# Fifteen computed softmax features per head in place of sixteen, in a linear-attention kernel

## The chip, the cores and the metric

The kernel runs on one core of one Trainium2 chip. TensorE (PE) does matrix products, VectorE (DVE), ScalarE (ACT) and GpSimd (POOL) work on rows of data, SyncE (SP) issues DMAs, and each engine takes its instructions in the order in which they were written for it. The metric is device time in microseconds.

## The reference

One sequence of 2048 rows of width 512 passes through two layers, each a linear attention and a gated MLP, with layer norms and residuals. What matters here is the feature map of the attention: 32 heads of 16 dimensions, and per head a softmax over 16 features of `q @ w_phi` and one over the negated values.

```python
pq = jnp.einsum("bhsd,hdf->bhsf", q, w_phi)
pk = jnp.einsum("bhsd,hdf->bhsf", k, w_phi)
phi_q = jnp.concatenate([_softmax(pq, axis=-1), _softmax(-pq, axis=-1)], axis=-1)
phi_k = jnp.concatenate([_softmax(pk, axis=-1), _softmax(-pk, axis=-1)], axis=-1)
kv = jnp.einsum("bhsf,bhsd->bhfd", phi_k, v)
z  = jnp.einsum("bhsf->bhf", phi_k)
num = jnp.einsum("bhqf,bhfd->bhqd", phi_q, kv)
den = jnp.einsum("bhqf,bhf->bhq", phi_q, z)[..., None] + 1e-6
o = num / den
```

Both layers use the same weights. The MLP is `(relu(x @ W_gate) * (x @ W_up)) @ W_down` with a width of 1376.

## The kernel before

The 2048 rows are 16 tiles of 128. Activations in bf16, weights and all intermediate tiles stay in SBUF. `w_phi` is folded into the key and query weights at the start (`fold`): `Wk2` and `Wq2` are the products of the projection and of a block-diagonal `Wblk`, so that one product per tile gives the logits of all 32 heads, 512 columns. A softmax does not change when a constant is subtracted from its logits, and `centre` subtracts the mean of `w_phi` over the features ahead of the fold.

**A key tile** (`Keys.begin`, `finish`, `scale`): four matmuls of 512 columns into a PSUM bank (line 571; the first tile of the first layer goes by another way, lines 562 and 567), two exponentials on ScalarE, of the logits and of their negatives, into a buffer `ek` (574), four matmuls for the values (577), one VectorE sum over groups of 16 into `sk` (582), logarithm and exponential of minus the logarithm on ScalarE as a reciprocal (591, 594), a scaling of the features in place by it, on POOL or VectorE (534), and eight matmuls `kvz` that add to the state, with features as weights and values as moving data (606).

**A query tile** (`query`): four matmuls of 512 columns (633), two exponentials (636), a sum into `sq` (639), logarithm and exponential (644, 646) of the positive half's sums only, the ratio of the negative sum to the positive one (650), on POOL or VectorE, a scaling of the positive half by it (654), on POOL or VectorE, and a transposing DMA on SP's queue into `fq`. The common factor of both halves cancels in num / den. `attend` then multiplies `fq` with the masked state `R` (670), divides (677 to 684), transposes, projects (693) and adds the residual (697). `mlp` follows (matmuls at 746, 770 and 810).

The order of the work isn't computed when the program is built: `ORDER` lists all steps in the order in which they are issued, `PLACE` says for each step that could run on two engines which it takes, `IDLE` puts in filler matmuls, and `SLOTS` gives the buffer of each tile that a step takes from a pool. `arrange` only replays them. There are 21 `ek` buffers for keys and queries alike, six PSUM banks `b`. The costs that stand beside each step aren't used when the lists are replayed. A step that overwrites a buffer waits for its last reader.

The program's parts follow each other loosely: constants and fold to some 10 us, keys and queries of the first layer to some 57 us, then attention and MLP of the first layer in blocks of tiles, with the second layer's keys and queries threaded in between to some 240 us, and the second layer's MLP to the end.

Of the kernel before, what the change touches and what calls it, by code (L numbers as in the profile page):

```python
# [8 lines left out]
P = 128  # L9
D = 512  # L10
# [13 lines left out]
GE = HG * (DH + 1)  # L24
EPS = 1e-5
# [117 lines left out]
class K:  # L143
# [24 lines left out]
)  # L168
IDLE = (
# [107 lines left out]
def kernel(  # L277
# [26 lines left out]
    Wk2, Wq2 = new("Wk2", [NB, D]), new("Wq2", [NB, D])  # L304
# [20 lines left out]
    p_ek = p_eq = pool("ek", 21, [NG, 2, GQ])  # L325
# [71 lines left out]
    c_id = op("POOL", (900, 900), 0, lambda: make_identity(nc, ident[:]), name="ident")  # L397
    c_eps = op("DVE", DVE0, 0, lambda: nc.vector.memset(eps[:], EPS), name="eps")
# [11 lines left out]
    def centre():  # L410
        nc.vector.tensor_reduce(out=cmean[:], in_=wf[:], axis=AX.X, op=Alu.add)
        nc.vector.scalar_tensor_tensor(out=wf[:], in0=cmean[:].unsqueeze(2).to_broadcast([P, NB, DH]),
                                       scalar=-1.0 / DH, in1=wf[:], op0=Alu.mult, op1=Alu.add)

    def blocks(e):
        e.tensor_tensor(
            out=Wblk[:].rearrange("p b (j f) -> p b j f", f=DH),
            in0=wf[:].unsqueeze(2).to_broadcast([P, NB, HB, DH]),
            in1=Mf[:].unsqueeze(1).unsqueeze(3).to_broadcast([P, NB, HB, DH]), op=Alu.mult)

    c_cen = op("DVE", (400, 500), 20, centre, [l_wf], name="wcen", port=True)
    c_blk = op("DVE", (640, 740), 20, lambda: blocks(nc.vector), [c_m, c_cen], name="Wblk", port=True,
               alt=("POOL", (1016, 1058), lambda: blocks(nc.gpsimd), 3))
    c_mg = op("DVE", DVE0, 15000, lambda: nc.vector.tensor_tensor(
        out=Mg[:], in0=Mf[:, 0:HG], in1=Mf[:, HG:HB], op=Alu.add), [c_m], name="Mg")
# [20 lines left out]
    def fold(w, dst, loaded, due, step, engs, by_dma=False):  # L446
# [17 lines left out]
        for m in range(NB):  # L464
            ps = Buf(p_b)
            f = op("PE", mm(4, 128), due + step + m, lambda m=m, ps=ps: [nc.tensor.matmul(
                ps.t[:, b * P:(b + 1) * P],
                lhsT=wT.t[:, m, b * P:(b + 1) * P] if by_dma else wT.t[:, b, m * P:(m + 1) * P], rhs=Wblk[:, b, :],
                start=True, stop=True) for b in range(NB)], [turned[m], c_blk], [ps], [wT], name="fold")
            done.append(evac(engs[m % 2], due + step + m, lambda m=m: dst[:, m, :], lambda ps=ps: ps.t[:], [f], (),  # L470
                             [ps], "W2"))
# [58 lines left out]
    def halves(name, ek, out, scale, engs, due, after, takes, uses):  # L530
        parts = []

        def phi(e, lo, n):
            e.tensor_tensor(  # L534
                out=out().rearrange("p g s (h f) -> p (g s h) f", f=DH)[:, lo:lo + n],
                in0=ek.t[:].rearrange("p g s (h f) -> p (g s h) f", f=DH)[:, lo:lo + n],
                in1=scale(lo, n).unsqueeze(2).to_broadcast([P, n, DH]), op=Alu.mult)
        for k, e in enumerate(engs):
            ways = {"DVE": ("DVE", dve(512), lambda k=k: phi(nc.vector, k * H, H), 1),
                    "POOL": ("POOL", (1016, 1058), lambda k=k: phi(nc.gpsimd, k * H, H), 3)}  # L540
            _, cost, f, _ = ways[e]
            parts.append(op(e, cost, due, f, after, [] if k else takes, uses + (takes if k else []), name=name,
                            port=ways[e][3], alt=ways["POOL" if e == "DVE" else "DVE"]))
        return parts

    class Keys:
# [9 lines left out]
        def begin(self, sk, row, t, due, due_v, due_z, xT, phi_eng, v_eng="ACT"):  # L556
# [3 lines left out]
            if self.l == 0 and t < PLAIN:  # L560
                kT, tp = Buf(p_gu), Buf(p_b)
                k = op("PE", (960, 1130, 16), due, lambda: [nc.tensor.matmul(
                    tp.t[:, e * P:(e + 1) * P], lhsT=wk[:, b, e * P:(e + 1) * P], rhs=xnTA[c][:, i, b, :],
                    start=(b == 0), stop=(b == NB - 1)) for e in range(NB) for b in range(NB)],
                    [xT] + l_wk, [tp], name="KT")
                k = evac("DVE", due, lambda: kT.t[:, 0, :], lambda: tp.t[:], [k], [kT], [tp], "kT")
                k = op("PE", mm(4, 128), due, lambda: [nc.tensor.matmul(
                    kp.t[:, b * P:(b + 1) * P], lhsT=kT.t[:, 0, b * P:(b + 1) * P], rhs=Wblk[:, b, :],
                    start=True, stop=True) for b in range(NB)], [k, c_blk], [kp], [kT], name="K")
            else:  # L570
                k = op("PE", mm(4, 512), due, lambda: [nc.tensor.matmul(  # L571
                    kp.t[:], lhsT=xnTA[c][:, i, b, :], rhs=Wk2[:, b, :], start=(b == 0), stop=(b == NB - 1))
                    for b in range(NB)], [xT] + k_fold, [kp], name="K")
            e = [op("ACT", act(512), due, lambda s=s: nc.scalar.activation(  # L574
                out=ek.t[:, :, s, :], in_=kp.t[:].rearrange("p (g e) -> p g e", e=GQ), func=AF.Exp, scale=1.0 - 2.0 * s), [k], [ek] if s == 0 else [],
# [7 lines left out]
                out=sk.t[:, row, :], in_=ek.t[:].rearrange("p g s (h f) -> p (g s h) f", f=DH), axis=AX.X, op=Alu.add),  # L583
# [5 lines left out]
        def finish(self, begun):  # L589
            n, sk, due = len(begun), begun[0][2], begun[-1][5]  # L590
            a = op("ACT", RLN[n - 1], due, lambda: nc.scalar.activation(
                out=sk.t[:, 0:n, :], in_=sk.t[:, 0:n, :], func=AF.Ln, scale=1.0), [b[0] for b in begun], (), [sk],
                name="lnk")
            a = op("ACT", REXP[n - 1], due, lambda: nc.scalar.activation(  # L594
                out=sk.t[:, 0:n, :], in_=sk.t[:, 0:n, :], func=AF.Exp, scale=-1.0), [a], (), [sk], name="rk")
            for row, b in enumerate(begun):
                self.scale(a, row, *b[1:])

        def scale(self, a, row, v, sk, ek, vx, due, due_z, phi_eng):
            a = halves("phi", ek, lambda: ek.t[:], lambda lo, n: sk.t[:, row, lo:lo + n], PHI[phi_eng], due, [a], [],  # L600
                       [ek, sk])

            def kvz():
                for g in range(NG):
                    b = g % NB
                    nc.tensor.matmul(self.bufs.t[:, g, 0:GV],  # L606
                                     lhsT=ek.t[:, g, :, :].rearrange("p s e -> p (s e)"), rhs=vx.t[:, g, 0:GV],
# [22 lines left out]
    def query(l, t, due, xT, behind, key):  # L630
        c, i = t // C, t % C
        qp, ek, sq, fq = Buf(p_a), Buf(p_eq), Buf(p_sq), Buf(p_fq)
        q = op("PE", mm(4, 512), due, lambda: [nc.tensor.matmul(  # L633
            qp.t[:], lhsT=xnTA[c][:, i, b, :], rhs=Wq2[:, b, :], start=(b == 0), stop=(b == NB - 1))
            for b in range(NB)], [xT] + q_fold, [qp, ek], name="Q", follow=key)
        e = [op("ACT", act(512), due, lambda s=s: nc.scalar.activation(  # L636
            out=ek.t[:, :, s, :], in_=qp.t[:].rearrange("p (g e) -> p g e", e=GQ), func=AF.Exp, scale=1.0 - 2.0 * s),
            [q], (), [qp, ek], name="Eq") for s in range(2)]
        a = op("DVE", SUM16, due, lambda: nc.vector.tensor_reduce(  # L639
            out=sq.t[:], in_=ek.t[:].rearrange("p g s (h f) -> p (g s h) f", f=DH), axis=AX.X, op=Alu.add),  # L640
# [4 lines left out]
            out=pos(), in_=pos(), func=AF.Ln, scale=1.0), [a], (), [sq], name="lnq")  # L645
# [3 lines left out]
        def ratio(e):  # L649
            e.tensor_tensor(out=pos(), in0=pos(), in1=neg(), op=Alu.mult)  # L650

        def scale(e):
            v = ek.t[:, :, 0, :].rearrange("p g (h f) -> p g h f", f=DH)
            e.tensor_tensor(out=v, in0=v, in1=pos().unsqueeze(3).to_broadcast([P, NG, HG, DH]), op=Alu.mult)  # L654
        a = op("POOL", (212, 253), due, lambda: ratio(nc.gpsimd), [a], [], [ek, sq], name="rat", port=3,
               alt=("DVE", DVE0, lambda: ratio(nc.vector), 1))
        a = op("POOL", (1016, 1058), due, lambda: scale(nc.gpsimd), [a], [], [ek, sq], name="phq", port=3,
               alt=("DVE", dve(512), lambda: scale(nc.vector), 1))
        a = op("SP", XWIDE, due, lambda: nc.sync.dma_start_transpose(
            out=fq.t[:], in_=ek.t[:].rearrange("p g s e -> p (g s e)")), [a], [fq], [ek], name="fq", move=1450)  # L660
# [268 lines left out]
```

## Time and profile before

| what | value |
|---|---|
| median of three timed runs | 374.3 us (373.25 to 374.6) |
| span of the profiled execution, first to last instruction | 371.3 us |
| median less that span (starting and ending work around it) | 3.0 us |
| granted TensorE clock | 1.000 |
| TensorE busy | 363.7 us |
| VectorE busy | 273.1 us |
| ScalarE busy | 201.8 us |
| POOL busy | 97.6 us |
| key matmuls, line 571 | 120 records, 30.6 us |
| query matmuls, line 633 | 122 records, 31.5 us |
| exponentials, lines 574 and 636 | 64 of 642 ns, 64 of 637 ns (mean) |
| logarithms, lines 591 and 644 | 32 of 319 ns, 32 of 252 ns (mean) |

The profiled execution has no total of its own beside its span, so the 3.0 us are the difference to the median of the timed runs. Busy is the time in which at least one instruction of an engine is under way. Instructions of one engine overlap, so that a mean duration can include waiting for the one ahead, and is longer than the time for which the engine is held. Some matmul records are missing from the trace: 124 key matmuls and 128 query matmuls of 512 columns were issued.

In the rows of the profile, `L571` is line 571 of the kernel before, `b<-Wk,xnTA` says that a tile of pool `b` is written from `Wk` and `xnTA`, `x120` is a count, and an arrow at the end names what ended the idle time ahead of an instruction.

### The profile page before, as it was taken

To read this page: it belongs to the slowest core of one execution; us is meant where nothing else is said; L and a number is where in the kernel's file an instruction comes from. 1 tells how busy PE (TensorE), PEld (TensorE's weight loads), DVE (VectorE), ACT (ScalarE), POOL (GpSimd) and SP (SyncE) were. 2 spreads that over 40 slices of the span, in tenths; PEclk is the share of its full clock that TensorE was granted. 3 is DMA by queue.
4 is the path that set the end of the run, shared out by engine and by line. 5 is a ranking of instruction groups with operands and counts; after the bars stand their busy time and mean duration, and the time that the engine had idled before them with its cause. 6 is when DMAs were issued, how large, how long until landed. Compare 5 with 4: busy or idle time off the path is not lost.

```text
span 371.3 us, 7447 instructions
## 1 busy us (share of the span) xinstructions
PE 363.7 (98%) x2799; PEld 217.4 (59%) x2845; DVE 273.1 (74%) x578; ACT 201.8 (54%) x549; POOL 97.6 (26%) x123
## 2 busy tenths in 40 slices
PE   8999999999999999999999999999999999999996
PEld 5454557776455454545566655687755454457484
DVE  6999999988798966849969489799976373233253
ACT  5999999661644750586274455874434226403130
POOL 4599974610030116005212174141000000000000
PEclk9999999999999999999999999999999999999999
DMA  8998676686653501203411210488851102010213
GB/s 247 185 236 154 230 129 128 128 158 116 92 99 58 99 15 31 40 18 64 87 31 34 57 28 3 58 131 125 142 104 45 28 0 44 0 45 0 79 52 98
DMA packets 93925, 31.73 MB, mean 85 GB/s; under 512 B 85345, under 2 KB 92865, under 8 KB 93889
## 3 DMA queue, kind: packets, MB, share of 16 engines
q1 hardware_dynamic: 93088, 30.98, 41.4%
q8 instruction: 22, 0.36, 0.4%
q10 hardware_dynamic: 800, 0.28, 0.3%
q14 instruction: 15, 0.11, 0.1%
HBM read 8.44 MB, written 2.10 MB: 28 GB/s over the span
## 4 chain that ended last, share of the span: by engine, by line
PE 85%; ACT 9%; DVE 2%; issue 1%; DMA 1%; POOL 0%; SPq 0%; DVEq 0%; ACTq 0%
PE b L770 38%; PE b L810 20%; PE b L693 7%; PE b L571 5%; PE b L577 5%; PE b L633 4%; ACT ek L574 3%; PE b L746 3%; PE q L670 2%; ACT ek L636 2%; PE q L606 1%; DMA X<-in_A_x_dram 1%; DVE ek L534 1%; PE b L485 1%; ACT vext L438 1%
## 5 line engine op out<-in xcount | busy, mean ns | idle before, releaser
L770 PE MATMUL b<-xnTB,wgu 128*128 128x128 bf16 (+2 forms) x1200 | 152.5, 279 | 0.1
L770 PEld LDWEIGHTS <-wgu 128*128 128x128 bf16 x1200 | 97.4, 98 | 47.2 <-issue 0.3
L774 ACT ACTIVATE gu<-b 128x512 bf16<-128x512 f32 (+1 forms) x83 | 47.7, 582 | 90.7 <-PE b L770 85.4
L810 PE MATMUL b<-wd,hT 128*128 128x512 bf16 (+3 forms) x342 | 83.5, 372 | 1.2
L534 POOL TENSOR_TENSOR ek<-ek,sk 128x512 bf16<-128x512 bf16 x48 | 52.1, 1109 | 74.1 <-ACT sk L594 69.4
L810 PEld LDWEIGHTS <-hT 128*128 128x128 bf16 (+1 forms) x363 | 34.2, 98 | 34.0 <-DVE hT L787 0.3
L787 DVE TENSOR_TENSOR hT<-gu,b 128x512 bf16<-128x512 bf16 (+1 forms) x44 | 28.6, 658 | 30.0 <-ACT gu L774 13.6
L574 ACT ACTIVATE ek<-b 128x512 bf16<-128x512 f32 x64 | 38.5, 642 | 9.1 <-PE b L571 8.9
L636 ACT ACTIVATE ek<-b 128x512 bf16<-128x512 f32 x64 | 37.5, 637 | 7.8 <-PE b L633 7.8
L639 DVE TENSOR_REDUCE sq<-ek 128x64 f32<-128x1024 bf16 x32 | 38.5, 1211 | 4.1 <-ACT ek L636 4.1
L582 DVE TENSOR_REDUCE sk<-ek 128x64 f32<-128x1024 bf16 x32 | 38.2, 1206 | 2.9 <-ACT ek L574 2.7
L654 POOL TENSOR_TENSOR ek<-ek,sq 128x512 bf16<-128x512 bf16 x26 | 27.8, 1077 | 43.8 <-DVE sq L650 33.1
L778 DVE TENSOR_TENSOR hT<-gu 128x512 bf16<-128x512 bf16 (+1 forms) x39 | 16.9, 435 | 22.5 <-ACT gu L789 22.5
L817 DVE SCALAR_TENSOR_TENSOR X<-b,rsB,X 128x512 bf16<-128x512 f32 (+2 forms) x33 | 23.7, 730 | 12.4 <-PE b L810 12.2
L693 PE MATMUL b<-wo,oT 128*128 128x512 bf16 x118 | 31.2, 379 | 1.1 <-ACT oT L438 0.4
L633 PE MATMUL b<-Wq,xnTA 128*128 128x512 bf16 x122 | 31.5, 379 | 0.4
L577 PE MATMUL b<-wv,xnTA 128*128 128x512 bf16 x123 | 31.1, 379 | 0.3
L571 PE MATMUL b<-Wk,xnTA 128*128 128x512 bf16 x120 | 30.6, 379 | 0.1
L697 DVE SCALAR_TENSOR_TENSOR X<-b,X 128x512 bf16<-128x512 f32 x32 | 21.8, 686 | 6.2 <-PE b L693 5.9
L789 ACT CAST gu<-b 128x512 bf16<-128x512 f32 (+1 forms) x39 | 21.9, 573 | 6.8 <-PE b L770 6.6
L684 DVE TENSOR_TENSOR o<-q,rd 128x512 bf16<-128x512 f32 x32 | 22.0, 687 | 1.3 <-ACT rd L681 0.8
L495 DVE BATCH_NORM_STATS2 bstA<-X 128x6 f32<-128x512 bf16 x32 | 21.5, 684 | 2.0 <-DMA X<-in_A_x_dram 1.7
(83 smaller groups left out, 357.9 us busy)
## 6 DMA issues: line engine op xcount, KB each, us to landing
out_dram<-X SPq DMA_DIRECT2D x15, 128.0 KB, 1.8
X<-in_A_x_dram SPq DMA_DIRECT2D x6, 256.0 KB, 4.9
wgu<-in_B_W_gate_dram SPq DMA_DIRECT2D x4, 344.0 KB, 3.7
wgu<-in_B_W_up_dram SPq DMA_DIRECT2D x4, 344.0 KB, 5.2
wd<-in_B_W_down_dram SPq DMA_DIRECT2D x5, 256.0 KB, 3.7
hT<-in_A_wqkv_dram SPq DMA_DIRECT2D x3, 256.0 KB, 4.2
X<-in_A_x_dram SPq DMA_DIRECT2D x4, 128.0 KB, 3.3
wv<-in_A_wqkv_dram SPq DMA_DIRECT2D x2, 256.0 KB, 4.8
```

Of the source, the lines that this page charges most:

```text
L534: e.tensor_tensor(out=out().rearrange("p g s (h f) -> p (g s h) f", f=DH)[:, lo:lo + n], in0=ek.t[:].rearrange("p g s (h f) -> p (g s h) f ...
L571: k = op("PE", mm(4, 512), due, lambda: [nc.tensor.matmul(kp.t[:], lhsT=xnTA[c][:, i, b, :], rhs=Wk2[:, b, :], start=(b == 0), stop=(b == ...
L574: e = [op("ACT", act(512), due, lambda s=s: nc.scalar.activation(out=ek.t[:, :, s, :], in_=kp.t[:].rearrange("p (g e) -> p g e", e=GQ), fu ...
L577: v = op("PE", mm(4, 512), due_v, lambda: [nc.tensor.matmul(vp.t[:], lhsT=xnTA[c][:, i, b, :], rhs=wv[:, b, :], start=(b == 0), stop=(b == ...
L582: a = op("DVE", SUM16, due, lambda: nc.vector.tensor_reduce(out=sk.t[:, row, :], in_=ek.t[:].rearrange("p g s (h f) -> p (g s h) f", f=DH) ...
L633: q = op("PE", mm(4, 512), due, lambda: [nc.tensor.matmul(qp.t[:], lhsT=xnTA[c][:, i, b, :], rhs=Wq2[:, b, :], start=(b == 0), stop=(b == ...
L636: e = [op("ACT", act(512), due, lambda s=s: nc.scalar.activation(out=ek.t[:, :, s, :], in_=qp.t[:].rearrange("p (g e) -> p g e", e=GQ), fu ...
L639: a = op("DVE", SUM16, due, lambda: nc.vector.tensor_reduce(out=sq.t[:], in_=ek.t[:].rearrange("p g s (h f) -> p (g s h) f", f=DH), axis=A ...
L693: a = op("PE", mm(4, 512), due + 3, lambda j=j, yp=yp: [nc.tensor.matmul(yp.t[:], lhsT=oT.t[:, j, b, :], rhs=wo[:, b, :], start=(b == 0), ...
L770: nc.tensor.matmul(ps.t[:, q * W:(q + 1) * W].rearrange("p (i t) -> p i t", t=P), lhsT=wgu[:, s, b, g * P:(g + 1) * P], rhs=xT.t[:, 0:n, b ...
L774: nc.scalar.activation(out=gu.t[:, 0, 0:cols], in_=gp.t[:, 0:cols], func=AF.Relu)
L810: nc.tensor.matmul(yp.t[:, 0:c1 - c0], lhsT=h.t[:m, f * W + i * P:f * W + (i + 1) * P], rhs=wd[:m, f, c0:c1], start=(f == 0), stop=(f == N ...
```

## The change

Of the 16 features of a softmax one can be made constant: with the last column of `w_phi` subtracted from the others, the last logit is 0 and its exponential 1. The kernel after computes only the other 15. `Wblk` has 120 columns per block, `Wk2` and `Wq2` have 480, a key or query product has 480 columns, the exponentials write 2 x 4 x 15 features per group of four heads, and the last 8 of the 128 places of a group hold the constant features.

The sums run over 15 features; the missing 1 is added as the bias of the logarithm, from a tile `unit`. For keys the reciprocal is written straight into the eight last places of each group (in bf16), since 1 times the scale is the scale, and the scaling of the other features reads it there. For queries the ratio is computed as (negative sum + 1) times the positive reciprocal, always on VectorE, and written into the four places of the positive half. The four places of the negative half must hold 1: POOL sets them once at the start, in 12 of the 21 `ek` buffers (9 to 20), and queries use these alone, as long as no key has used them before. So the `ek` entries of `SLOTS` are other ones. `ORDER`, `PLACE` and `IDLE` are as before. The masks `Mg` of the state follow the new layout.

```diff
+DF = DH - 1
+GF = HG * DF
+FW = H * DF
...
+ONES = tuple(range(9, 21))
...
-    c_id = op("POOL", (900, 900), 0, lambda: make_identity(nc, ident[:]), name="ident")
+    def first_constants():
+        make_identity(nc, ident[:])
+        for i in ONES:
+            nc.gpsimd.memset(p_eq.tiles[i][:, :, 2 * GF + HG:P], 1.0)
+    c_id = op("POOL", (900, 900), 0, first_constants, name="ident")
...
-        nc.vector.tensor_reduce(out=cmean[:], in_=wf[:], axis=AX.X, op=Alu.add)
-        nc.vector.scalar_tensor_tensor(out=wf[:], in0=cmean[:].unsqueeze(2).to_broadcast([P, NB, DH]),
-                                       scalar=-1.0 / DH, in1=wf[:], op0=Alu.mult, op1=Alu.add)
+        nc.vector.tensor_tensor(out=wf[:, :, 0:DF], in0=wf[:, :, 0:DF],
+                                in1=wf[:, :, DF:DH].to_broadcast([P, NB, DF]), op=Alu.subtract)
...
+        def phi(e, lo):
+            v = features(ek, lo, n)
+            e.tensor_tensor(out=v, in0=v, in1=ek.t[:, lo:lo + n, 2 * GF:P].unsqueeze(3).to_broadcast(
+                [P, n, 2 * HG, DF]), op=Alu.mult)
...
+    def raised(ek, ps, s, side):
+        assert side == "K" or ek.slot in ONES and ek.slot not in spoilt
+        if side == "K":
+            spoilt.add(ek.slot)
+        nc.scalar.activation(out=ek.t[:, :, s * GF:(s + 1) * GF], in_=ps.t[:, 0:FW].rearrange(
+            "p (g e) -> p g e", e=GF), func=AF.Exp, scale=1.0 - 2.0 * s)
...
-                    kp.t[:], lhsT=xnTA[c][:, i, b, :], rhs=Wk2[:, b, :], start=(b == 0), stop=(b == NB - 1))
+                    kp.t[:, 0:FW], lhsT=xnTA[c][:, i, b, :], rhs=Wk2[:, b, :], start=(b == 0), stop=(b == NB - 1))
...
+                out=sk.t[:, 0, :], in_=sk.t[:, 0, :], func=AF.Ln, scale=1.0, bias=unit[:]), [done, c_eps], (), [sk],
...
+                out=ek.t[:, :, 2 * GF:P], in_=sk.t[:, 0, :].rearrange("p (g j) -> p g j", g=NG), func=AF.Exp,
+                scale=-1.0), [a], (), [sk, ek], name="rk")
...
-        def ratio(e):
-            e.tensor_tensor(out=pos(), in0=pos(), in1=neg(), op=Alu.mult)
+        def ratio():
+            nc.vector.scalar_tensor_tensor(out=ek.t[:, :, 2 * GF:2 * GF + HG], in0=neg(), scalar=1.0, in1=pos(), op0=Alu.add,
+                                   op1=Alu.mult)
...
-        a = op("POOL", (212, 253), due, lambda: ratio(nc.gpsimd), [a], [], [ek, sq], name="rat", port=3,
-               alt=("DVE", DVE0, lambda: ratio(nc.vector), 1))
+        a = op("DVE", DVE0, due, ratio, [a], [], [ek, sq], name="rat", port=1, alt=("DVE", DVE0, ratio, 1))
```

More of the change, by code (lines that the diff above doesn't have):

```diff
@@ L303 @@
     wv, wo = new("wv", [NB, D]), new("wo", [NB, D])
-    Wk2, Wq2 = new("Wk2", [NB, D]), new("Wq2", [NB, D])
+    Wk2, Wq2 = new("Wk2", [NB, FW]), new("Wq2", [NB, FW])
     wf = new("wf", [NB, DH])
@@ L307 @@
     ident = new("ident", [P])
-    Mf, Mg = new("Mf", [HB], F32), new("Mg", [HG], F32)
-    Wblk = new("Wblk", [NB, P])
-    cmean = new("cmean", [NB], F32)
+    Mf, Mg, Mh = new("Mf", [HB], F32), new("Mg", [HG], F32), new("Mh", [HG], F32)
+    Wblk = new("Wblk", [NB, HB * DF])
     R = new("R", [NG, GE])
     xnTA = [new(f"xnTA{c}", [C, NB, P]) for c in range(C)]
-    eps = new("eps", [1], F32)
+    eps, unit = new("eps", [1], F32), new("unit", [1], F32)
     rowsum, ssq = new("rowsum", [2, T], F32), new("ssq", [2, T], F32)
@@ L324 @@
     p_xn = pool("xn", 3, [2, D])
-    p_ek = p_eq = pool("ek", 21, [NG, 2, GQ])
+    p_ek = p_eq = pool("ek", 21, [NG, P])
+    spoilt = set()
     p_sk = pool("sk", 4, [2, 2 * H], F32)
@@ L582, in begin @@
             a = op("DVE", SUM16, due, lambda: nc.vector.tensor_reduce(
-                out=sk.t[:, row, :], in_=ek.t[:].rearrange("p g s (h f) -> p (g s h) f", f=DH), axis=AX.X, op=Alu.add),
+                out=sk.t[:, row, :].rearrange("p (g j) -> p g j", g=NG), in_=features(ek), axis=AX.X, op=Alu.add),
                 e, [] if row else [sk], [ek, sk] if row else [ek], name="sk")
```

105 lines of the change are left out of this document (53 added, 52 removed).

## The prediction

> **What bounds the kernel now.** I read the page first, then busy time by stage, then the chain of work that ended last.
>
> ```profile
> span 371.3 us, 7447 instructions
> ...
> PE 363.7 (98%) x2799; PEld 217.4 (59%) x2845; DVE 273.1 (74%) x578; ACT 201.8 (54%) x549; POOL 97.6 (26%) x123
> ...
> PE 85%; ACT 9%; DVE 2%; issue 1%; DMA 1%; POOL 0%; SPq 0%; DVEq 0%; ACTq 0%
> ```
>
> The chain is 85% TensorE, so the obvious reading is that fewer matmul columns save time one for one. The stages qualify it. The columns are PE, PEld, DVE, ACT and POOL busy, then clock and DMA:
>
> ```profile
> 19.26:44.67 25.41, 25.08 (x187) 13.10 (x189) 25.41 (x34) 25.38 (x74) 24.07 (x25) 1.00 0.89 219
> 44.67:56.90 12.23, 11.71 (x117) 6.59 (x116) 12.03 (x16) 11.81 (x36) 9.38 (x12) 1.00 0.66 112
> 56.90:72.00 15.10, 14.71 (x203) 11.77 (x207) 14.55 (x33) 12.59 (x41) 7.69 (x11) 1.00 0.61 127
> 72.00:210.00 138.00, 137.21 (x899) 79.56 (x911) 107.87 (x228) 71.03 (x192) 27.95 (x30) 1.00 0.38 69
> ```
>
> From 19 to 45 us, where the first layer's keys and queries are made, VectorE (25.41 of 25.41) and ScalarE (25.38) are as full as TensorE. After 72 us only TensorE is. The pieces of the chain (start, length, what) agree:
>
> ```profile
> 17.49 1.74 PE b L571 x8
> ...
> 19.26 2.06 ACT ek L574 x4
> ...
> 44.74 0.56 POOL sq L650
> ...
> 56.92 1.04 PE b L693 x4
> ...
> 87.22 0.86 PE b L571 x4
> 88.08 0.86 PE b L693 x4
> ...
> 132.12 1.32 PE b L746 x16
> ```
>
> Every piece of the chain from 19.26 until the POOL piece at 44.74 is ScalarE's, one behind the other. From there to 56.9 it runs through POOL, VectorE and ScalarE, and from 56.92 on it is matmuls that touch (87.22 + 0.86 is 88.08). So the change is priced by ScalarE first, by TensorE later.
>
> **TensorE.** A 512-column matmul takes 0.86 / 4 = 215 ns, a 192-column one (two runs of 96) 1.32 / 16 = 82.5 ns: 0.41 ns a column, so 32 columns less save 13.3 ns. By the loops each layer has 16 key and 16 query tiles of four matmuls; the second layer's all run after 72 us: 32 x 4 x 13.3 ns = -1.7 us on a chain of touching matmuls. The first layer's would save as much again (one key tile is made another way), but they run mostly under ScalarE's chain. The loop counts, the order of each engine's work and SP's queue are the same in both programs, except that the ratio moves to VectorE.
>
> **ScalarE.** The exponentials shrink, but each of the 64 logarithms gains a bias read from the tile `unit`. Its only relative in the trace is the logarithm of the normalisation, which already reads `eps`:
>
> ```profile
> 16.15 0.31 ACT L503 ACTIVATE lnA<-mvA,eps 128x2 f32<-128x2 f32 x1
> 16.34 0.62 ACT L574 ACTIVATE ek<-b 128x512 bf16<-128x512 f32 x1
> ...
> 16.81 0.23 ACT L505 ACTIVATE rsA<-lnA 128x2 f32<-128x2 f32 x1
> 16.91 0.32 ACT L503 ACTIVATE lnA<-mvA,eps 128x2 f32<-128x2 f32 x1
> ```
>
> On a full ScalarE the next instruction starts 0.19 us behind the one with a bias tile (16.15 to 16.34) and 0.10 us behind its twin of the same size without one (16.81 to 16.91). So a bias tile holds the engine 0.09 us longer. What an exponential saves comes from two sizes of one operation:
>
> ```profile
> 61.40 0.60 ACT L774 ACTIVATE gu<-b 128x512 bf16<-128x512 f32 x1 [0.17 <-PE b L770]
> ...
> 63.24 0.39 ACT L774 ACTIVATE gu<-b 128x256 bf16<-128x256 f32 x1
> ```
>
> 0.21 us for 256 elements, so 32 fewer save 0.026 us. The counts in ScalarE's stretch of the chain:
>
> ```profile
> L574 ACT ACTIVATE ek<-b 128x512 bf16<-128x512 f32 x24 | 15.4, 710 | 0.0
> L636 ACT ACTIVATE ek<-b 128x512 bf16<-128x512 f32 x11 | 7.3, 797 | 0.0
> L591 ACT ACTIVATE sk<-sk 128x64 f32<-128x64 f32 x11 | 4.5, 428 | 0.0
> ...
> L644 ACT ACTIVATE sq<-sq 128x32 f32<-128x32 f32 x2 | 1.0, 492 | 0.0
> ```
>
> 35 exponentials x 0.026 = -0.9 us, 13 logarithms x 0.09 = +1.2 us, three folded weights (480 columns) -0.1: **+0.2 us**. In the stage where TensorE's columns were to pay first, ScalarE, which sets the end, gets slightly longer. Ahead of 19.26 the chain is TensorE's, with a piece of 8 key matmuls; ScalarE stands close behind, so I take -0.1 (0 to -0.3).
>
> From 44.67 to 56.9 ScalarE has these logarithms:
>
> ```profile
> L644 ACT ACTIVATE sq<-sq 128x32 f32<-128x32 f32 x5 | 1.2, 249 | 0.4 <-DVE sq L639 0.3
> ...
> L591 ACT ACTIVATE sk<-sk 128x64 f32<-128x64 f32 x3 | 0.7, 273 | 0.0
> ```
>
> 8 x 0.09 = +0.7, less its idle time there (12.23 - 11.81 = 0.4): at most +0.3.
>
> **VectorE and POOL.** The sums read 960 elements in place of 1024, and the ratio, 24 times on POOL and 8 times on VectorE until now, is VectorE's alone:
>
> ```profile
> L582 DVE TENSOR_REDUCE sk<-ek 128x64 f32<-128x1024 bf16 x32 | 38.2, 1206 | 2.9 <-ACT ek L574 2.7
> ...
> L411 DVE TENSOR_REDUCE cmean<-wf 128x4 f32<-128x64 bf16 x1 | 0.2, 212 | 0.0
> ```
>
> ```profile
> L650 POOL TENSOR_TENSOR sq<-sq x24: 247/252/768, 44.7 to 257.9; 128x32 f32<-128x32 f32 x24
> ...
> L650 DVE TENSOR_TENSOR sq<-sq x8: 128/186/941, 58.7 to 190.9; 128x32 f32<-128x32 f32 x8
> ```
>
> ```profile
> L650 POOL TENSOR_TENSOR sq<-sq 128x32 f32<-128x32 f32 x10 | 3.3, 330 | 5.0 <-ACT sq L646 4.8
> ```
>
> (1206 - 212) / 960 is 1.04 ns an element, so a sum saves 66 ns: 64 x 66 = -4.2 us over the run. The 24 ratios that leave POOL cost VectorE 24 x 0.186 = +4.5 us: an even exchange in total, but the sums are spread and the ratios come from 44.7 us on, ten of them by 72 us (the last row is the stretch from 8 to 72). If half of these fall before 56.9, VectorE gets +0.9 there, less the shorter sums. On the chain a POOL ratio of 0.56 gives way to one of 0.19. Between -0.4 and +0.3 (ScalarE's too) I take 0 for this stretch.
>
> The moved ratio is a new wait on VectorE: it must have the reciprocal from ScalarE, and sums, residuals and MLP products queue behind it, and TensorE for those. I set each of the 32 places in the new order against the trace; in 29 the reciprocal is there first, typically as below; in the other three VectorE would wait up to 0.7 us where it already stood idle for longer.
>
> ```profile
> 62.09 0.69 DVE L684 TENSOR_TENSOR o<-q,rd 128x512 bf16<-128x512 f32 x1
> 62.15 0.23 ACT L646 ACTIVATE sq<-sq 128x32 f32<-128x32 f32 x1
> ```
>
> The reciprocal ends at 62.38, VectorE comes free at 62.78: no wait. The cover is 0.4 us; where it is gone, the shortfall is VectorE's.
>
> POOL's scalings go from 512 to 480 elements, now in rows of 15 and with a bf16 factor:
>
> ```profile
> L534 POOL TENSOR_TENSOR ek<-ek,sk 128x512 bf16<-128x512 bf16 x48 | 52.1, 1109 | 74.1 <-ACT sk L594 69.4 <-DVE vext L439 2.4 <-DVE xn L519 2.3
> ```
>
> By the 32-element ratio (252 ns) and this row the slope is 1.8 ns, so -57 ns each; this hides under ScalarE (POOL 24.07 of 25.41). The new row form is in no trace; bounds are that saving and a lengthening priced below.
>
> **Buffers and start.** Queries now keep to ek buffers 9 to 20 and keys reuse the low ones sooner. The tightest of the early key reuses is this:
>
> ```profile
> 37.90 0.68 PE L606 MATMUL q<-vext,ek 128*128 128x65 bf16 x16
> ...
> 39.31 0.87 ACT L574 ACTIVATE ek<-b 128x512 bf16<-128x512 f32 x1
> ```
>
> The exponential at 39.31 overwrites a buffer whose last reader is among the matmuls that end at 38.58: 0.7 us to spare, so no cost as long as POOL is not later. At the start POOL gets 12 small memsets in front of this:
>
> ```profile
> 4.30 0.19 POOL L515 TENSOR_SCALAR nm<-mvA 128x1 f32<-128x1 f32 x1 [2.99 <-DVE mvA L496]
> ```
>
> Even at 0.247 us each (the smallest ratio) they fit in the 2.99 us for which POOL waits. I take 0.
>
> **Sum.** -0.1 (to 19.26) + 0.2 (to 44.67) + 0 (to 56.9) + 0 (to 72, bounds as before) - 1.7 (after) = -1.6 us on the profiled span: 369.7. The three timed runs have a median of 374.3, 3.0 us over that span; these 3 us stay. **372.7 us**, 0.4% less, inside the 0.5% that a measurement of this kernel can tell from no change.
>
> **Rivals.** *All columns pay.* If ScalarE's and VectorE's orders have more give than 25.4 of 25.4 shows, the first layer's (16 x 4 + 15 x 4) x 13.3 ns = -1.7 come too: 374.3 - 3.3 = 371.0. For it: the chain ahead of 19.26 and TensorE's own fullness. Against: ScalarE's unbroken stretch.
>
> *TensorE has hidden slack.* If the matmuls after 72 us only look dense, their 1.7 us vanish in gaps: 374.4. The touching pieces of 215 ns speak against it. The Trainium skill, page "Perfetto Trace Analysis", section "Identifying the Most-Contended Engine", says that matmul busy time misleads, since pipelined matmuls look smaller, and would have the 98% distrusted. By that rule the sum is 374.4; the start-to-start times above bear it out no further.
>
> *The ratio meets POOL* (slower). A VectorE instruction with two inputs from SBUF can be held until POOL's running one is done:
>
> ```profile
> 139.66 3.53 POOL L534 TENSOR_TENSOR ek<-ek,sk 128x512 bf16<-128x512 bf16 x3
> ...
> 141.28 0.94 DVE L650 TENSOR_TENSOR sq<-sq 128x32 f32<-128x32 f32 x1
> ```
>
> Here a ratio took 0.94 in place of 0.19. The ten POOL ratios that move between 44.7 and 72 us come where VectorE has only 0.2 + 0.55 us idle. Held 0.75 each, they add 7.5 - 0.75 = +6.8, with -1.6 from the sum: 379.5. It decides for slower, over 376.2, from 0.43 us each. Against: the median of the eight is 0.186, and a query's own scaling cannot run ahead of its ratio. The Trainium skill, page "GPSIMD Engine Reference", section "Key points", says that POOL shares its SBUF interfaces with VectorE and contends with instructions of two SBUF inputs; this row agrees.
>
> *Rows of 15 cost POOL.* At 1.4 us a scaling in place of 1.1, some 20 among POOL's 25 instructions of the full stage add 6.0, of which 1.3 is idle: 377.4 with the sum. It decides for slower from 0.24 us each. No row shows such a form, for or against.
>
> **How the numbers follow.** Forecast 0.50 (371.8 to 373.6), all columns 0.21, hidden slack 0.14, ratio meets POOL 0.10, rows of 15 0.05. Faster by over 0.5% means under 372.4: two fifths of the forecast's range and the all-columns case, 0.20 + 0.21 = 0.41. Slower: 0.15. Within: 0.44. The range takes in all columns with 0.4 us of scatter below, and above the slack case and the mild end of the holds: 370.6 to 375.4.
>
> **What would show it.** Key and query matmuls near 202 ns apart; ScalarE still full from 19 to 45 us with logarithms about 0.09 us longer; sums near 1.14 us; VectorE's ratios near 0.19 us; the chain TensorE's from 57 us on, reaching 72 us of before within 0.5 us and gaining steadily behind. Wrong it would be if POOL's scalings exceed 1.1 us, ratios take 0.4 us or more, or the 57 us mark is 1 us earlier.

## The result, and the profile after

| | before | after |
|---|---|---|
| median of 8 runs each on one chip | 373.91 us (373.04 to 374.63) | 371.81 us (371.62 to 372.70) |
| ratio | 1 | 0.9948 (95%: 0.9932 to 0.9965) |
| span of the profiled execution | 371.3 us | 370.0 us |
| time of that execution | not given | 371.77 us |

The changed kernel is 0.5% faster. The forecast was 372.7 us, within 0.5% of no change as its likeliest case, and a range from 370.6 to 375.4.

Of after, time and span of the same execution are known: 371.77 - 370.0 = 1.8 us around the span, not the 3.0 us that the prediction took from a median. The executions of before fall in two groups, 372.8 to 373.9 and 374.2 to 375.2 us, and the profile of before (371.3 + 1.8 = 373.1) is of the lower one. The median of before, 373.91 us, lies between the groups, where no execution lies. Profile against profile the change is worth 1.3 us, and the fastest execution of each kernel gives 1.4 (373.04 to 371.62); medians, which mix the groups, show 2.1.

The page of the changed kernel, its span, busy times and the chain's shares:

```profile
span 370.0 us, 7444 instructions
...
PE 361.4 (98%) x2803; PEld 217.0 (59%) x2845; DVE 272.0 (74%) x604; ACT 203.4 (55%) x549; POOL 86.6 (23%) x111
...
PE 84%; ACT 9%; DVE 2%; issue 1%; DMA 1%; POOL 1%; SPq 0%; DVEq 0%; ACTq 0%
```

POOL lost 11.0 us of work (97.6 to 86.6), VectorE only 1.1 us. The same three stages as in the prediction, with the same columns:

```profile
19.26:44.67 25.41, 24.81 (x187) 12.97 (x189) 25.18 (x35) 25.38 (x74) 22.59 (x25) 1.00 0.91 218
44.67:56.90 12.23, 11.09 (x115) 6.39 (x114) 12.03 (x20) 11.88 (x36) 7.27 (x7) 1.00 0.71 111
56.90:72.00 15.10, 14.62 (x203) 11.73 (x207) 14.69 (x37) 13.02 (x42) 6.04 (x6) 1.00 0.63 128
```

ScalarE is as full as before from 19 to 45 us (25.38), and VectorE from 45 to 57 us (12.03 of 12.23), while TensorE has 0.6 us less to do there. There the gain of the columns became idle time of TensorE. The groups of the changed steps (L568 are the exponentials, L606 and L661 the sums, L615 and L666 the logarithms, L672 the ratio, L554 and L677 POOL's scalings):

```profile
L568 ACT ACTIVATE ek<-b 128x480 bf16<-128x480 f32 x128 | 69.9, 597 | 16.1 <-PE b L596 8.6 <-PE b L656 6.1 <-issue 1.3
L554 POOL TENSOR_TENSOR ek<-ek 128x480 bf16<-128x480 bf16 x48 | 49.5, 1055 | 79.2 <-ACT ek L618 74.6 <-DVE ek L554 2.3 <-DVE xn L534 2.3
...
L606 DVE TENSOR_REDUCE sk<-ek 128x64 f32<-128x960 bf16 x32 | 36.0, 1138 | 2.5 <-ACT ek L568 2.5
...
L677 POOL TENSOR_TENSOR ek<-ek 128x480 bf16<-128x480 bf16 x26 | 26.4, 1023 | 73.7 <-DVE ek L672 55.9 <-ACT gu L797 9.7 <-issue 7.4
...
L615 ACT ACTIVATE sk<-sk,unit 128x64 f32<-128x64 f32 x32 | 11.9, 382 | 5.8 <-DVE sk L606 5.8
...
L666 ACT ACTIVATE sq<-sq,unit 128x32 f32<-128x32 f32 x32 | 10.6, 336 | 2.8 <-DVE sq L661 2.5
L672 DVE SCALAR_TENSOR_TENSOR ek<-sq 128x32 bf16<-128x32 f32 x32 | 7.9, 251 | 1.2 <-ACT sq L668 0.8
```

The sums take 1.14 us as forecast, the logarithms 0.06 and 0.08 us more than before in the mean (382 and 336 in place of 319 and 252), the scalings 1.06 and 1.02 us. The ratio takes 182 ns in the median, near the 186 assumed (itself a median), but 251 ns in the mean, since three of the 32 took far longer. The chain of waits of the changed kernel shows one of them:

```profile
28.89 0.81 PE b L656 x4
...
47.22 0.04 DVE ek L672
47.25 0.85 issue
...
57.90 0.40 PE b L500 x4
...
72.53 0.86 PE b L833 x4
```

A query tile's four matmuls take 0.81 us in place of 0.86, 202 ns each. The 72 us mark (72.53 against 72.51, the same piece in both) has not moved. At 47.22 the chain meets a ratio and then 0.85 us of "issue", time for which the profile shows nothing that VectorE waited for. The timeline of VectorE and POOL at that place:

```profile
47.22 0.97 DVE L672 SCALAR_TENSOR_TENSOR ek<-sq 128x32 bf16<-128x32 f32 x1
...
47.14 0.99 POOL L554 TENSOR_TENSOR ek<-ek 128x480 bf16<-128x480 bf16 x1 [1.26 <-ACT ek L618]
```

The ratio lasts until POOL's scaling, begun 0.08 us ahead of it, is done (47.14 + 0.99 = 48.13). Two more of the 32 ratios are held so (0.88 us at 140.67 and 0.98 at 184.32); the one at 140.67 was VectorE's in before already, and held (0.94 us at 141.28). The meeting itself is not new either. In before the ratio of 47.22 was POOL's, and it took 0.73 us in place of 0.25 beside a scaling of VectorE's (from 47.11 to 47.79):

```profile
47.17 0.73 POOL L650 TENSOR_TENSOR sq<-sq 128x32 f32<-128x32 f32 x1 [0.53 <-ACT sq L646]
```

So the change moved the hold from POOL, which is busy for 9.38 of the 12.23 us of that stage, to VectorE, which is full there.

To see where the lead over before arises, I set each ScalarE instruction against the one with the same number in before's trace (both have 549). Differences in us; the columns are the time in before, and a number in brackets is that of an experiment below:

| kernel | 16.3 | 48.6 | 73.8 | 237.3 | 258.3 | 358.4 |
|---|---|---|---|---|---|---|
| after | -0.10 | 0.02 | 0.02 | -1.67 | -1.29 | -1.29 |
| first layer wide (1) | -0.05 | 0.18 | 0.30 | -1.40 | -1.07 | -1.03 |
| second layer wide (2) | 0.38 | 0.50 | 0.40 | 0.20 | 0.48 | 0.62 |
| immediate bias (3) | -0.29 | -1.21 | -0.39 | -2.21 | -1.90 | -1.89 |
| before with bias tile (4) | -0.06 | 1.17 | 0.97 | 1.11 | 1.27 | 1.43 |
| after again (5) | -0.31 | -0.15 | -0.14 | -1.79 | -1.50 | -1.50 |
| ratio behind the sum (6) | -0.20 | -0.04 | -0.41 | -2.10 | -1.74 | -1.75 |
| ratio on POOL (7) | -0.23 | -0.11 | -0.64 | -2.37 | -2.41 | -2.16 |
| three edits (8) | 0.64 | -0.08 | -0.36 | -2.18 | -1.60 | -1.46 |
| POOL ratio with its 1 (9) | -0.02 | -0.66 | 0.27 | -1.55 | -1.59 | -1.58 |
| product from PSUM (10) | 0.45 | 0.57 | 0.57 | -1.13 | -0.55 | -0.56 |
| before, second profile (11) | 0.84 | 0.84 | 0.95 | 0.94 | 1.06 | 1.27 |
| before, third profile (12) | 0.10 | 0.07 | 0.12 | 0.12 | 0.29 | 0.44 |

Two profiles of one kernel differ by 0.1 to 0.2 us in most columns (after and 5; before and 12), and 11 by more, so a smaller difference between two rows says little.

After gains nothing by 74 us and 1.69 us from there to 237, then gives 0.38 back by 258. At that place TensorE's weight loads wait for a transposing DMA, and the SyncE queue shows its issue:

```profile
253.91 2.52 PEld L793 LDWEIGHTS <-wgu 128*128 128x128 bf16 x24 [0.17 <-DMA xnTB<-xn]
...
248.91 1.23 SPq L495 DMA_TRANSPOSE xnTB<-xn  x1
```

In before no wait stands at that load. VectorE, which feeds that DMA, is busy for 17.11 of the 18 us from 238 to 256, against 16.33 before (the stage in after, then in before):

```profile
238.00:256.00 18.00, 17.80 (x246) 14.77 (x247) 17.11 (x38) 12.33 (x41) 4.01 (x4) 1.00 0.83 122
```

```profile
238.00:256.00 18.00, 17.79 (x254) 14.71 (x256) 16.33 (x34) 12.50 (x43) 5.49 (x9) 1.00 0.73 107
```

One of its MLP products (two SBUF inputs) is held by POOL as well, first after, then before:

```profile
244.01 0.85 DVE L801 TENSOR_TENSOR hT<-gu 128x512 bf16<-128x512 bf16 x1
```

```profile
245.69 0.49 DVE L778 TENSOR_TENSOR hT<-gu 128x512 bf16<-128x512 bf16 x1
```

### The profile page after: what moved, and what is told of

Read it like the earlier page. It is cut to its first block, busy times and chain, and to the rows that moved or that the text cites. A ratio compares the mean times of both kernels' runs of the same rounds, so it can differ in the third digit from the quotient of the medians.

```text
span 370.0 us, 7444 instructions
## 1 busy us (share of the span) xinstructions
PE 361.4 (98%) x2803; PEld 217.0 (59%) x2845; DVE 272.0 (74%) x604; ACT 203.4 (55%) x549; POOL 86.6 (23%) x111
## 4 chain that ended last, share of the span: by engine, by line
PE 84%; ACT 9%; DVE 2%; issue 1%; DMA 1%; POOL 1%; SPq 0%; DVEq 0%; ACTq 0%
PE b L793 38%; PE b L833 20%; PE b L716 7%; ACT ek L568 4%; PE b L601 4%; PE b L596 4%; PE b L656 4%; PE b L769 3%; PE q L693 2%; PE q L629 1%; ACT vext L453 1%; DMA X<-in_A_x_dram 1%; DVE sq L661 1%; ACT sk L615 1%; PE b L500 1%
## 5 line engine op out<-in xcount | busy, mean ns | idle before, releaser
L568 ACT ACTIVATE ek<-b 128x480 bf16<-128x480 f32 x128 | 69.9, 597 | 16.1 <-PE b L596 8.6
L554 POOL TENSOR_TENSOR ek<-ek 128x480 bf16<-128x480 bf16 x48 | 49.5, 1055 | 79.2 <-ACT ek L618 74.6
L677 POOL TENSOR_TENSOR ek<-ek 128x480 bf16<-128x480 bf16 x26 | 26.4, 1023 | 73.7 <-DVE ek L672 55.9
L661 DVE TENSOR_REDUCE sq<-ek 128x64 f32<-128x960 bf16 x32 | 36.4, 1144 | 4.1 <-ACT ek L568 4.1
L606 DVE TENSOR_REDUCE sk<-ek 128x64 f32<-128x960 bf16 x32 | 36.0, 1138 | 2.5 <-ACT ek L568 2.5
L656 PE MATMUL b<-Wq,xnTA 128*128 128x480 bf16 x128 | 30.5, 365 | 0.1
L596 PE MATMUL b<-Wk,xnTA 128*128 128x480 bf16 x124 | 29.5, 366 | 0.0
L601 PEld LDWEIGHTS <-xnTA 128*128 128x128 bf16 x128 | 12.0, 98 | 12.7 <-issue 0.3
```

The costliest lines, as they stand in the source:

```text
L554: e.tensor_tensor(out=v, in0=v, in1=ek.t[:, lo:lo + n, 2 * GF:P].unsqueeze(3).to_broadcast([P, n, 2 * HG, DF]), op=Alu.mult)
L568: nc.scalar.activation(out=ek.t[:, :, s * GF:(s + 1) * GF], in_=ps.t[:, 0:FW].rearrange("p (g e) -> p g e", e=GF), func=AF.Exp, scale=1.0 ...
L596: k = op("PE", mm(4, FW), due, lambda: [nc.tensor.matmul(kp.t[:, 0:FW], lhsT=xnTA[c][:, i, b, :], rhs=Wk2[:, b, :], start=(b == 0), stop=( ...
L601: v = op("PE", mm(4, 512), due_v, lambda: [nc.tensor.matmul(vp.t[:], lhsT=xnTA[c][:, i, b, :], rhs=wv[:, b, :], start=(b == 0), stop=(b == ...
L606: a = op("DVE", SUM16, due, lambda: nc.vector.tensor_reduce(out=sk.t[:, row, :].rearrange("p (g j) -> p g j", g=NG), in_=features(ek), axi ...
L656: q = op("PE", mm(4, FW), due, lambda: [nc.tensor.matmul(qp.t[:, 0:FW], lhsT=xnTA[c][:, i, b, :], rhs=Wq2[:, b, :], start=(b == 0), stop=( ...
```

## The experiments

In the rows of a run, L571 and the like are lines of that run's own kernel.

**1 and 2: which columns pay.** `wide = D if l == 0 else FW` (or `l == 1`) for the key and query matmuls, with zero columns in `Wk2` and `Wq2`; nothing else changes.

```diff
-            qp.t[:, 0:FW], lhsT=xnTA[c][:, i, b, :], rhs=Wq2[:, b, :], start=(b == 0), stop=(b == NB - 1))
+            qp.t[:, 0:wide], lhsT=xnTA[c][:, i, b, :], rhs=Wq2[:, b, 0:wide], start=(b == 0), stop=(b == NB - 1))
```

> The kernel after, with the key and query matmuls of the first layer at 512 columns again (32 columns of zero weights, whose results nobody reads); ScalarE, VectorE and POOL still work on 480. Theory (ScalarE sets the end of the first stage): TensorE's 1.65 us there are idle time anyway, so the time stays within 0.3 us of the kernel after, 371.8 us, and the matmuls at 57 to 60 us start where they do in the kernel after. Rival (all columns pay, the rest is a coincidence of other costs): 1.65 us more, 373.5 us.

> The same, with the second layer's key and query matmuls at 512 columns in place of the first's. Theory (TensorE sets the pace from 57 us on): 128 matmuls x 13.3 ns = 1.7 us come back by 237 us, of which 0.35 us had been lost again between 244 and 258 us, so 1.3 to 1.7 us more than the kernel after: 373.1 to 373.5 us, that is no gain over the kernel before. Rival (hidden slack on TensorE): within 0.3 us of 371.8 us.

Measured: 372.15 us for the first layer (ratio 0.9964, 0.9949 to 0.9978), 0.3 more than after and just outside the theory's 0.3; 373.31 for the second (0.9992, 0.9979 to 1.0005), 1.5 more, as its theory said. In the table the first is 0.28 behind after at 74 us (0.44 behind the second profile of after) and stays so; the second gains 0.20 from 74 to 237 us where after gains 1.69. So 1.5 of the 1.7 us of the second layer are real, and some 0.3 of the first layer's, little more than two profiles of one kernel differ by. Neither *hidden slack* nor *all columns pay* holds.

Runs 1 to 4, 5 to 8 and 9 to 12 were timed on three chips, each set beside before, whose fastest execution was 372.8 to 373.0 us on each.

**3 and 4: the bias tile.**

```diff
-                out=sk.t[:, 0, :], in_=sk.t[:, 0, :], func=AF.Ln, scale=1.0, bias=unit[:]), ...
+                out=sk.t[:, 0, :], in_=sk.t[:, 0, :], func=AF.Ln, scale=1.0, bias=1.0), ...
```

and the same for the queries' logarithm; in 4, before's 64 logarithms get `bias=zero[:]` from a tile of zeros.

> The kernel after, with the 1 of the 64 logarithms as a constant in the instruction in place of the tile unit. Theory (the bias tile eats the gain of the first stage): the logarithms are 0.09 us shorter, 13 of them in the full stretch of ScalarE and 8 up to 57 us, so the first stage ends 1.0 to 1.5 us earlier (TensorE's own saving there is the limit) and the time is 370.3 to 370.8 us. Rival (VectorE, POOL or the buffers bind the first stage as well): under 0.4 us less, 371.4 to 371.8 us.

> The kernel before, with a bias tile that holds 0 on its 64 key and query logarithms; the results are the same. Theory: 13 x 0.09 = 1.2 us more in ScalarE's full stretch and up to 0.7 more by 57 us, nothing later, where TensorE sets the pace: 1.2 to 1.9 us slower than the kernel before, all of it there by 57 us. Rival (ScalarE's orders have give): under 0.4 us.

Measured: 370.81 us (0.9925, 0.9904 to 0.9946) and 374.63 us (1.0024, 1.0009 to 1.0039). The groups of the logarithms, in 3 and then in 4:

```profile
L615 ACT ACTIVATE sk<-sk 128x64 f32<-128x64 f32 x32 | 9.2, 300 | 5.9 <-DVE sk L606 5.9
...
L666 ACT ACTIVATE sq<-sq 128x32 f32<-128x32 f32 x32 | 7.8, 247 | 4.2 <-DVE sq L661 4.1
```

```profile
L594 ACT ACTIVATE sk<-sk,zero 128x64 f32<-128x64 f32 x32 | 12.8, 417 | 6.3 <-DVE sk L585 5.4 <-DVE rsB L736 0.9
...
L647 ACT ACTIVATE sq<-sq,zero 128x32 f32<-128x32 f32 x32 | 11.2, 353 | 2.8 <-DVE sq L642 2.8
```

With a tile 98 and 101 ns more than before (319 and 252), with an immediate no more at all. The Trainium skill, "ScalarE: Activation LUTs", section "What ACT_TABLE_LOAD costs", says that each per-partition pointer operand adds about 93 ns to an activation and an immediate none; both rows agree. On the path, in before, the tile costs 1.2 us by 48.6 us and still 1.0 at 74: ScalarE does set the end there. Over the whole run 4 it is 1.4 us by the spans (372.7 to 371.3) and 1.1 by the medians (before: 373.55 in that set), near the theory's 1.2 to 1.9 and far from the rival's 0.4. In after, the immediate gains 1.2 us by 48.6 but only 0.4 is left at 74 in this trace. The medians give more, 0.9 to 1.0 us (370.81 beside 371.69 and 371.81), the upper end of the theory's range: the profiled execution, 371.20 us, is the slowest of its six. Where the rest of the gain arises no trace shows. The stage from 44.67 to 56.9 us of run 3, and its VectorE and POOL there, show who takes over:

```profile
44.67:56.90 12.23, 10.63 (x114) 6.24 (x114) 12.20 (x20) 10.60 (x34) 7.17 (x7) 1.00 0.74 138
```

```profile
46.20 0.98 DVE L672 SCALAR_TENSOR_TENSOR ek<-sq 128x32 bf16<-128x32 f32 x1
...
45.75 1.38 POOL L554 TENSOR_TENSOR ek<-ek 128x480 bf16<-128x480 bf16 x1 [0.69 <-remote]
```

VectorE is full (12.20 of 12.23), with the held ratio among its work.

**5 to 8: the moved ratio.** 5 is after unedited. 6 puts one entry of the written order, the held ratio at 47.22, two places later, behind the sum that followed. 7 gives the 24 ratios back to POOL, without the added 1:

```diff
+        def ratio_pool():
+            nc.gpsimd.tensor_tensor(out=ek.t[:, :, 2 * GF:2 * GF + HG], in0=pos(), in1=neg(), op=Alu.mult)
-        a = op("DVE", DVE0, due, ratio, [a], [], [ek, sq], name="rat", port=1, alt=("DVE", DVE0, ratio, 1))
+        a = op("POOL", (212, 253), due, ratio_pool, [a], [], [ek, sq], name="rat", port=3, alt=("DVE", DVE0, ratio, 1))
```

8 joins 3 (and `bias=EPS` in the normalisation), 6, and the product of experiment 10.

> The changed kernel, unedited, beside the next three. Both theories: 371.6 to 372.0 us. They differ in the trace. Theory (the lead is given back by a fixed chain of waits): again 1.6 to 1.7 us ahead of before at 237 us and only about 1.3 ahead from 258 us on, with the MLP product at 244 us held at about 0.85 us and TensorE waiting about 0.17 us for the transposed activations at 253.9 us. Rival (that was one execution's chance): the lead at 258 us is 1.6 or more.

> VectorE's ratio that took 0.97 us at 47.22 us (POOL's scaling ran from 47.14 to 48.13) is put behind the sum that followed it, so that it starts when that scaling is done; nothing else moves. Theory (VectorE sets the end between 47 and 58 us, so the hold is on the path): the ratio takes about 0.18 us, TensorE's piece at 57.90 us starts 0.5 to 0.8 us earlier, and the end comes 0.5 to 0.8 us earlier: 371.0 to 371.3 us beside 371.8. Rival (another engine sets that stretch, the hold is free): the piece moves by less than 0.2 us, 371.6 to 371.9 us.

> The 24 ratios that the change took from POOL to VectorE go back to POOL, written as a plain product of two 32-column factors into the same 15th column (the added 1 of the constant feature's numerator is left out, so the output differs). Theory (the move is an even exchange, as predicted): VectorE loses five ratios between 44 and 58 us (0.97 + 4 x 0.18 us), but each query waits for a POOL ratio of 0.25 to 0.33 us and for the scalings of 1.0 us queued ahead of it; the piece at 57.90 us moves by -0.6 to +0.4 us, the time is 371.2 to 372.2 us. Rival 1 (the move cost time): the end comes 0.8 us or more earlier, 371.0 us or less. Rival 2 (the move paid): the end comes 0.5 us or more later, 372.3 us or more.

> The changed kernel with three edits: biases of the 64 logarithms (1.0) and of the normalisation's 20 logarithms (epsilon) written as immediates; the ratio held at 47.22 us put behind the next sum; the MLP product held at 244.01 us taken straight from PSUM instead of from a copy. Theory (the costs sit on the path one behind the other): -0.6 to -1.0 us for the biases, -0.8 for the ratio since VectorE is then full (12.20 of 12.23 us in that stretch of the run with immediate biases), -0.2 to -0.4 for the product: 369.6 to 370.3 us. Rival (the next limit takes over at once, POOL's scalings or the transposing DMAs): 370.5 us or more.

| run | median of 6 | ratio (95%) |
|---|---|---|
| 5 after again | 371.69 us (371.55 to 372.33) | 0.9942 (0.9924 to 0.9961) |
| 6 ratio behind the sum | 371.47 us (371.24 to 372.07) | 0.9935 (0.9916 to 0.9954) |
| 7 ratio on POOL | 371.15 us (370.91 to 371.36) | 0.9926 (0.9906 to 0.9946) |
| 8 three edits | 370.73 us (370.27 to 371.62) | 0.9916 (0.9896 to 0.9936) |

5: the lead again shrinks between 237 and 258 us, by 0.29 (0.38 in the first profile), and the MLP product is held again (0.85 us at 243.88). The expected wait of 0.17 us for the transposed activations isn't there: TensorE's load at 253.70 shows no wait over 0.1 us. 6 gains 0.2 us by the medians, though its six executions overlap those of 5, and 0.27 to 0.43 in the table at 74 us (against 5 and after), less than the 0.5 to 0.8 expected. The ratio is short, but the next limit is near:

```profile
48.02 0.18 DVE L661 SCALAR_TENSOR_TENSOR ek<-sq 128x32 bf16<-128x32 f32 x1
```

```profile
44.67:56.90 12.23, 11.53 (x118) 6.54 (x116) 11.49 (x21) 12.04 (x37) 6.92 (x7) 1.00 0.71 117
```

VectorE now has 0.74 us of give (11.49) and ScalarE is the fuller one (12.04). 7 is 0.5 us faster than 5, and no run of 7 is as slow as the fastest of 5. Its 371.15 us lies between the even exchange (371.2 or more) and rival 1 (371.0 or less): the move cost some 0.5 us, not 0.8. By the table 0.50 of it is there at 74 us, and it gives nothing back between 237 and 258 us (-2.37, -2.41), though 0.25 later. In that trace the chain from 42.92 to 53.44 is ScalarE's but for 0.05 us; with the ratio of 47.22 the chain of after runs through VectorE and POOL. VectorE from 238 to 256 us, and the product of 244 us:

```profile
238.00:256.00 18.00, 18.00 (x252) 14.89 (x250) 16.68 (x35) 12.50 (x40) 5.73 (x10) 1.00 0.85 122
```

```profile
243.35 0.42 DVE L804 TENSOR_TENSOR hT<-gu 128x512 bf16<-128x512 bf16 x1
```

TensorE is busy without a gap (18.00 of 18.00; 17.80 in after). 8 missed its range, and the rival's bound (370.5 or more) was met. It is the lowest median measured, though not to be told from 3 (370.81); 3 and 8 leave nothing of the computation out and are faster than both kernels. Its profiled execution (371.62 us, the slowest of the six) began 0.64 late, with TensorE waiting for the value weights:

```profile
11.13 1.89 PE L590 MATMUL b<-wv,xnTA 128*128 128x512 bf16 x8 [0.94 <-DMA wv<-in_A_wqkv_dram]
```

**9 and 10: a full ratio on POOL, and the held product.** 9 is 3 and 7 with `nc.gpsimd.tensor_scalar(... scalar1=1.0, op0=Alu.add)` on the numerator ahead of POOL's product. 10 is after with one `1` for a `0` in the written choices: the second factor of the product of 244.01 is read from PSUM, without ScalarE's copy.

> The changed kernel with its 24 moved ratios back on POOL, now with the added 1 (a second POOL instruction of 32 elements a query ahead of the product), and the 64 logarithms' bias of 1 as an immediate. Theory (both costs lie on the path, and one more short POOL instruction hides): 371.15 of the run with ratios on POOL, less 0.4 to 0.9 for the biases: 370.2 to 370.8 us. Rival (POOL's extra instruction of about 0.25 us, three to five of them in the stretch from 44 to 58 us, eats the gain): 371.0 us or more.

> The changed kernel, with the one MLP product that was held at 244.01 us reading its second factor straight from PSUM (ScalarE's copy ahead of it goes). Theory (that hold, by way of the residual and the transposing DMA, is what gives the lead back between 244 and 258 us): TensorE no longer waits 0.17 us each at 248 and 253.9 us, the lead over before at 258 us is 1.5 to 1.7 us in place of 1.3, and the time 0.2 to 0.4 us less than the changed kernel's 371.7 to 371.8. Rival (the two ratios in VectorE's queue alone give it back): the lead at 258 us stays at 1.3, the time within 0.1 us.

9: 371.44 us (0.9932, 0.9914 to 0.9951), the rival's case. It leads by 0.66 at 48.6 us and is 0.27 behind at 74. POOL's extra instruction lies on the path; all three rows below are pieces of the chain that ended last:

```profile
43.80 0.77 POOL L676 TENSOR_SCALAR sq<-sq 128x32 f32<-128x32 f32 x1
...
45.95 0.69 POOL L676 TENSOR_SCALAR sq<-sq 128x32 f32<-128x32 f32 x1
46.73 0.25 POOL L677 TENSOR_TENSOR ek<-sq 128x32 bf16<-128x32 f32 x1
```

0.77 and 0.69 us, where the median of the 24 is 0.29, beside two scalings of VectorE's (from 43.77 and 45.40 us): the hold works both ways. Between 237 and 258 us this run gives nothing back, like 7.

10: 371.93 us of five runs (0.9948, 0.9929 to 0.9966), no gain. The hold is gone, but the lead shrinks by 0.58 between 237 and 258 us, more than in after. VectorE, TensorE's weight loads and SyncE's queue:

```profile
243.86 0.68 DVE L810 TENSOR_TENSOR hT<-gu,b 128x512 bf16<-128x512 bf16 x1
244.45 0.18 DVE L672 SCALAR_TENSOR_TENSOR ek<-sq 128x32 bf16<-128x32 f32 x1
...
254.65 2.41 PEld L793 LDWEIGHTS <-wgu 128*128 128x128 bf16 x23 [0.27 <-DMA xnTB<-xn]
...
248.42 1.33 SPq L495 DMA_TRANSPOSE oT<-o  x1
249.85 1.28 SPq L495 DMA_TRANSPOSE xnTB<-xn  x1
```

The product, at 243.86, now stands ahead of a query's ratio, which is later for it; its scaling, and the transposing DMAs behind it in SyncE's queue, are later too, so that the DMA TensorE waits for is issued only when SyncE comes free of the one ahead (248.42 + 1.33 = 249.75). So taking the hold away alone doesn't keep the lead; 8 carries this edit too, and loses the same 0.58 there. In the table every run with all ratios on VectorE gives back 0.28 to 0.58 us between 237 and 258 us, the two with ratios on POOL (7 and 9) nothing, and before's own profiles differ there by 0.12 to 0.17. That the moved ratios give the lead back is shown by that; the way from them to the late DMA is argued, since in 7 and 9 the ratios are gone from VectorE's queue and the product isn't held either (0.42 and 0.46 us).

**11 and 12: before once more.**

> The kernel before, unedited, for a second profile of it: its executions lie in two groups, 372.8 to 373.8 and 374.2 to 375.2 us, and the profile that the prediction was made from (span 371.3) belongs with the lower. Theory (the groups part in the first 58 us, where VectorE, ScalarE and POOL are full and a late load or a held instruction decides): a profile of the upper group shows about +1.3 us by the 57 us mark and touching matmuls behind as in the first. Rival (they part late, or in what lies around the span): equal marks to 72 us, the gap later.

> As the run before it, a third profile of the kernel before, since which group an execution falls into is not ours to set. Same theories: about +1.3 us by the 57 us mark if it is of the upper group, none if of the lower; rival: the groups part later.

Measured: 374.37 us (span 372.6) and 373.51 us (span 371.7), so one of each group, and 1.8 us around the span in both. 12 is within 0.12 of the first profile up to 237 us and 0.44 behind at the end. 11 is 0.84 us behind at 16 us already and keeps that (1.3 was expected by 57 us); a further 0.4 comes behind 48 us. First before, then 11, TensorE's first value matmuls:

```profile
10.20 1.89 PE L577 MATMUL b<-wv,xnTA 128*128 128x512 bf16 x7
```

```profile
11.04 1.89 PE L577 MATMUL b<-wv,xnTA 128*128 128x512 bf16 x7 [0.75 <-DMA wv<-in_A_wqkv_dram]
```

The theory (first 58 us, a late load) holds for two thirds of the difference. That after falls into such a group more seldom is not shown.

## Why the prediction came out as it did

- **What bounds the stages**: right. ScalarE 25.38 of 25.41, TensorE's chain from 57 us on, the 72 us mark within 0.02 us. Run 2 shows TensorE's bound at work, run 4 ScalarE's.
- **-1.7 after 72 us**: right in size (1.69 by 237 us; run 2 puts it at 1.5), but not kept: 0.3 to 0.4 is given back by 258 us. The prediction looked at gaps in before alone, where the transposing DMA landed just as TensorE came to need it. TensorE ran 1.67 ahead, VectorE and that DMA only 1.4.
- **-0.1, +0.2, 0 and 0 up to 72 us**: the sum, +0.1, was right by luck (0.02 measured, -0.14 in run 5), since its terms were not. At the 74 us mark the bias tiles cost 0.25 to 0.4 us (run 3 against 5 and after), the moved ratios 0.5 to 0.65 (run 7 against 5 and after), and the first layer's columns brought 0.3 to 0.4 (run 1), not nothing. What brought the rest back, the shorter exponentials and sums or something else, no run shows. Within ScalarE's own stretch the price of the tile was right: 13 x 0.09 = 1.2 us, and 1.2 measured by 48.6 us in 3 and in 4.
- **"An even exchange in total"**: this step failed. In total it was even (VectorE's busy time went from 273.1 to 272.0 us), but the path was not: one held ratio of 0.97 us fell into the 12 us in which VectorE is the bound. That one is worth 0.2 to 0.4 us (run 6), all moved ratios together 0.5 to 0.65 at 74 us (run 7), where the prediction took 0. *The ratio meets POOL* had the mechanism and not the size: three of 32 were held, two of them moved ones, instead of ten. The argument against it, that a query's scaling cannot run ahead of its own ratio, missed that POOL scales keys (L554 at 47.14) and other queries meanwhile. The Trainium skill, "GPSIMD Engine Reference", section "Key points", has this contention; the row at 47.22 agrees, and run 9 shows it in POOL's direction.
- **Rows of 15**: cost nothing; POOL's scalings take 1055 and 1023 ns in place of 1109 and 1077, near the 57 ns less that were forecast.
- **"These 3 us stay"**: wrong, it is 1.8 us. A span of 370.0 in place of 369.7 and 1.2 us too much around it give the 0.9 us between 372.7 and 371.8. So the two errors partly cancel, and the closeness of the total is in part luck.
- **The chances**: the part of the range under 372.4 us, 0.6 of 1.8, is a third and not two fifths; faster by over 0.5% would then be 0.38 in place of 0.41, which changes nothing here.

## What to carry to other kernels

Price each stage by the engine that is full there: the same 32 columns were worth 1.5 us in one layer and 0.3 us in the other. A constant that can be an immediate should not be a tile on an engine that sets the end. When work moves from POOL to VectorE, set each moved two-input instruction against POOL's work at its place, since holds in the full stretch can outweigh an exchange that is even in total; and take the time around a span from an execution that has both.

## What was not expected of the hardware

The wait goes both ways. VectorE's ratios of 0.18 us lasted 0.88 to 0.98 us in after where POOL's scaling was under way (at 47.22 until 48.19, the scaling until 48.13), and POOL's instructions of 32 elements took 0.73 us in before (47.17) and 0.77 in run 9 beside VectorE's scalings, in place of 0.25 and 0.29. A load that TensorE waits 0.75 us for in the first 11 us (run 11) stays in the time to the end; in run 8 a wait of 0.94 us for it is, with its other edits, made up by 74 us (-0.36 there, beside -0.39 in run 3).
